# Moving the output bank's evacuation from two half copies on ACT to one copy on ACT and three moves on POOL

## The chip, the cores and the metric

The kernel runs on one core of one Trainium2 chip. The metric is the device time of one execution in microseconds (us), lower is better. Engines are named as the profile names them: PE (matmuls) with PEld (its weight loads), DVE, ACT, POOL, and SP, which issues most DMAs.

## The reference

Three stages follow each other. The first is attention inside clusters, for 2 batches, 8 heads, 768 positions and 64 dimensions per head; the other two are feed-forward layers (512 to 2048 to 512) on the 1536 tokens that come out of it.

```python
q_assign = np.argmax(np.einsum('bhsd,hcd->bhsc', q_n, c_n), axis=-1)   # 16 centroids a head
k_assign = np.argmax(np.einsum('bhsd,hcd->bhsc', k_n, c_n), axis=-1)
mask = q_assign[:, :, :, None] == k_assign[:, :, None, :]
scores = scale * np.matmul(q, k.transpose(0, 1, 3, 2))
scores = np.where(mask, scores, -1000000000.0)
attn = np.exp(scores - np.max(scores, axis=-1, keepdims=True))
attn = attn / (np.sum(attn, axis=-1, keepdims=True) + 1e-09)
x = np.matmul(attn, v)                       # to (tokens, heads * dims)
h = x @ w_in;    x = (h * np.cos(h)) @ w_out
h = x @ w2_in;   y = np.where(h >= 1, h, np.where(h <= -1, 0, (h + 1)**2 / 4)) @ w2_out
```

## The kernel before

Numbers are kept to more than one matmul pass of precision by splitting each fp32 operand into a high part and a low part, so most results are sums of two or three matmuls.

**Pairs, units and slots.** The attention stage works on 8 pairs `i` (a batch and two neighbouring heads). A pair has four units `u = 4 i + 2 h + hf` (head `h`, half `hf` of the 768 query rows), and a unit has six slots, one for each block of 128 keys: 192 slots in all. In its slot a unit transposes the exponentials of one key block on PE (`p_transpose`, L521), ACT copies the high part (`phi`, L524) and DVE makes the low part (`plo`, L529). The scores run `LEAD` = 8 slots ahead: two matmuls per slot (L475, L478), every second slot a row maximum on DVE (`nm`, L484) and an exponential on ACT (`p`, L493). The product with V (`p_v`, L539 and L540) accumulates in the single PSUM bank of `ps_o`; the six blocks are multiplied in the slots 4, 4, 5, 6, 7 and 8 after the unit's first.

**The output bank.** V is stacked as [high | low] for head 0 and [low | high] for head 1, so 64 rows of the bank hold the high product (`main`) and 64 the low one (`other`). After a unit's last product, `o_parts` copies each half on ACT into `xt0` and `xt1`, at the rows of that head (L553). The next unit cannot start its product until both copies have run, as the bank is the only one. After the second head, `finish` (two slots later) transposes the broadcast reciprocals `rb` on PE into `r` (L563), adds `xt0` and `xt1` on POOL (L565), multiplies by `r` on DVE (L566), and POOL splits the product into `xh` (L569) and, two slots later, `xl` (L573). `inverse` (L503 to L508) makes the reciprocals of a unit's sums and spreads each of three columns over 64 columns of `rb` with one POOL instruction a column.

**Preparation of a pair.** `prep_pair(i)` is a generator; the slot loop takes one step of it per slot. Its steps are: transposes of q and k (L331), copies of them on ACT and splits on POOL (L339, L303, L304), DMAs on SP that stack them for the scores (L317), the products with the centroids (L369, L370), their sum (L358), and the argmax chain: maximum (L416), compare (L418), weighting on POOL (L419), maximum (L424), compare (L426). The last step splits V on POOL (L439, L440), transposes the one-hot result on PE into `po` (L449), copies it on ACT (`oht`, L451) and puts eight DMAs on SP (L294) that write it into the stacked operands. The last step runs 5 slots after the previous pair's first; the first step 12 slots before that pair's first slot, because `PREP` is 12 and the generator takes 17 steps to get there.

**Shared buffers and order.** `pt`, `r`, `po`, `ptq` and `pd` all take their PSUM banks from a ring of three (`ps_t`). The order on each engine is not the order of the program text: a scheduler places every instruction from its own estimate of durations, by program order among those that it thinks ready, so the order of the neighbours shifts when a step is moved. `later(n, f)` calls `f` at the n-th next slot boundary.

**The feed-forward layers** take over PE as soon as the last product of the attention stage is done. Their SBUF pool takes the space of the attention pool, so its first writers wait for the last readers of that pool; the second weight block is converted in a chain over ACT, DVE and POOL (L144 to L160) into that space.

Of the kernel before, what the change touches and what calls it, by code (L numbers as in the profile page):

```python
# [8 lines left out]
F32 = mybir.dt.float32  # L9
# [4 lines left out]
AF = mybir.ActivationFunctionType  # L14
ALU = mybir.AluOpType
# [3 lines left out]
P = 128  # L19
# [13 lines left out]
def attention_moe_moe(  # L33
# [18 lines left out]
    nc = tc.nc  # L52
    B, H, S, D = q.shape
# [4 lines left out]
    HJ = NJ // 2  # L58
    HS = S // 2
# [9 lines left out]
    cpool = ctx.enter_context(tc.tile_pool(name="cpool", bufs=1))  # L69
# [2 lines left out]
    desc = cpool.tile([P, C], F32, name="desc")  # L72
    for c in range(C):
        nc.gpsimd.memset(desc[:, c:c + 1], float(C - c))
    ones = cpool.tile([P, D], F32, name="ones")
    nc.gpsimd.memset(ones, 1.0)
    ohscale = cpool.tile([P, 1], F32, name="ohscale")
    ohbias = cpool.tile([P, 1], F32, name="ohbias")
    for r in range(4):
# [25 lines left out]
    def later(n, f, *args):  # L105
        due.setdefault(now[0] + n, []).append((f, args))
# [85 lines left out]
    with ExitStack() as actx:  # L192
        ap = actx.enter_context(tc.tile_pool(name="apool", bufs=1))
# [19 lines left out]
        def ins(x):  # L213
            return x.ins if hasattr(x, "ins") else x

        def run_idle(n, after=None):

            with tc.issue_after(after) if after is not None else ExitStack():
                for _ in range(n):
                    nc.tensor.matmul(idle_o, idle[:, :P], idle, start=True, stop=True)  # L220
# [57 lines left out]
        def prep_pair(i):  # L278
# [3 lines left out]
            t = nat[i][0]  # L282
            if i in (1, 3, 5):
                t2 = w0pool.tile([P, 2, 2, S], F32R, tag="w_0", name=f"t2_{i}")
# [78 lines left out]
            for s in range(2):  # L363
                pd = ps_t.tile([P, NJ, 2, 2, C], F32, tag="t", name=f"pd{i}_{s}")
                for j in range(NJ):
                    cols = slice(j * P, (j + 1) * P)
                    o = pd[:, j].rearrange("p t h c -> p (t h c)")
# [11 lines left out]
            if i == 0:  # L379
                run_idle(NIDLE[2], ins(mm))  # L380
                for s in range(2):
                    dv = dotv[s]
                    m = mx[:, s * G // 2:(s + 1) * G // 2].rearrange("p (j h) -> p j h", h=2)
                    e = eq[:, s * G // 2:(s + 1) * G // 2].rearrange("p (j h) c -> p j h c", h=2)
                    mb = m.unsqueeze(3).to_broadcast([P, NJ, 2, C])
                    db = desc.unsqueeze(1).unsqueeze(1).to_broadcast([P, NJ, 2, C])
                    nc.vector.tensor_reduce(m, dv, AX.X, ALU.max)
                    nc.vector.tensor_tensor(e, dv, mb, ALU.is_ge)
                    nc.vector.tensor_tensor(e, e, db, ALU.mult)
                    nc.vector.tensor_reduce(m, e, AX.X, ALU.max)  # L390
                    nc.vector.tensor_tensor(dv, e, mb, ALU.is_equal)

                    po = ps_t.tile([P, HJ, P], F32, tag="t", name=f"po0_{s}")
                    for jp in range(HJ):
                        mm = nc.tensor.transpose(
                            po[:4 * C, jp],
                            dv[:, 2 * jp:2 * jp + 2].rearrange("p r h c -> p (r h c)"), ident)
                    run_idle(NIDLE[3 + s], ins(mm))
                    last_po[0] = ins(mm)
                    for h in range(2):  # L400
                        for par in range(2):
                            r0 = par * 2 * C
                            dst = st[h][s][D:D + 2 * C, 1].rearrange(
                                "c (jp par n) -> c jp par n", par=2, n=P)[:, :, par]
                            src = po[r0:r0 + 2 * C]
                            if s == 0:
                                nc.scalar.activation(dst, src, AF.Copy)
                            else:
                                nc.vector.tensor_scalar(
                                    dst, src, own[r0:r0 + 2 * C, 0, h:h + 1],  # L410
                                    own[r0:r0 + 2 * C, 1, h:h + 1], ALU.mult, ALU.add)
            else:
                dv = dots.rearrange("p j s h c -> p (j s h) c")
                mb = mx.unsqueeze(2).to_broadcast([P, G, C])
                yield
                nc.vector.tensor_reduce(mx, dv, AX.X, ALU.max)  # L416
                yield
                nc.vector.tensor_tensor(eq, dv, mb, ALU.is_ge)  # L418
                nc.gpsimd.tensor_tensor(  # L419
                    eq, eq, desc.unsqueeze(1).to_broadcast([P, G, C]), ALU.mult)  # L420
                yield
                yield
                yield
                nc.vector.tensor_reduce(mx, eq, AX.X, ALU.max)  # L424
                yield
                nc.vector.tensor_tensor(dv, eq, mb, ALU.is_equal)  # L426
                yield
            if i == 0:
                with tc.issue_after(ins(last[0])):
# [22 lines left out]
            for h in range(2):  # L452
                for s in range(2):
                    for par in range(2):
                        r0 = par * 64 + s * 32 + h * C
                        dst = st[h][s][D:D + C, 1].rearrange(
                            "c (jp par n) -> c jp par n", par=2, n=P)[:, :, par]
# [41 lines left out]
        def inverse(u):  # L499

            i, h, hf = units[u]
            den = dens.pop(u)
            nc.gpsimd.tensor_scalar(den[:, :, 0], den[:, :, 0], 1e-9, 1.0, ALU.add, ALU.mult)  # L503
            nc.vector.reciprocal(den[:, :, 1], den[:, :, 0])
            if h == 0:
                rb[(i, hf)] = ap.tile([P, HJ, 2, D], F32, tag="rb", bufs=2, name=f"rb{i}_{hf}")
            for jj in range(HJ):
                nc.gpsimd.tensor_scalar(rb[(i, hf)][:, jj, h], ones, den[:, jj, 1:2], 1.0,  # L508
                                        ALU.mult, ALU.mult)

        dens = {}
        rb = {}
        pts = {}
        xt = {}
# [29 lines left out]
        def o_parts(u):  # L544
            i, h, hf = units[u]
            o = opsum.pop(u)
            main = slice(h * D, (h + 1) * D)
            other = slice((1 - h) * D, (2 - h) * D)
            if h == 0:
                xt[(i, hf)] = [ap.tile([P, HS], F32, tag=f"xt{n}", bufs=2,  # L550
                                       name=f"xt{n}_{i}_{hf}") for n in range(2)]
            for t, rows in zip(xt[(i, hf)], (main, other)):
                nc.scalar.activation(t[main], o[rows], AF.Copy)  # L553
            if h == 1:
                later(2, finish, i, hf)

        def finish(i, hf):
            b, hp = pairs[i]
            t1, t2 = xt.pop((i, hf))
            r = ps_t.tile([P, HS], F32, tag="t", name=f"r{i}_{hf}")  # L560
            rbt = rb.pop((i, hf))
            for jj in range(HJ):
                nc.tensor.transpose(r[:, jj * P:(jj + 1) * P],  # L563
                                    rbt[:, jj].rearrange("p h d -> p (h d)"), ident)
            nc.gpsimd.tensor_tensor(t1, t1, t2, ALU.add)  # L565
            nc.vector.tensor_tensor(t2, t1, r, ALU.mult)  # L566
            c0 = b * S + hf * HS
            hi, lo = xh[:, hp, c0:c0 + HS], xl[:, hp, c0:c0 + HS]
            nc.gpsimd.tensor_scalar(hi, t2, 1.0, 0.0, ALU.mult, ALU.add)  # L569
            later(2, x_lo, lo, t2, hi)  # L570
# [4 lines left out]

        LEAD, PREP, PREP1 = 8, 12, -3
        PV_AT = (4, 4, 5, 6, 7, 8)
        NSLOT = len(units) * NJ  # L580
        PAIR = 4 * NJ
# [5 lines left out]
        for _ in prep_pair(0):  # L587
            next_slot()
# [9 lines left out]
        for slot in range(-max(LEAD, PREP), NSLOT + PV_AT[-1] - NJ + 1):  # L598
            g = slot + LEAD
            if slot in prep_at:  # L600
                preps.append(prep_pair(prep_at[slot]))
            if 0 <= slot < NSLOT:
                p_transpose(slot // NJ, slot % NJ)
            if 0 <= g < NSLOT:
                scores(g // 2, g % 2)
            for u, kt in pv_slots.get(slot, ()):
                p_v(u, kt)
            if slot % 2 == 0:
                for s in (slot - 1, slot):
                    if 0 <= s < NSLOT:  # L610
                        p_lo(s // NJ, s % NJ)
                if 2 <= g < NSLOT + 2:
                    row_exp(g // 2 - 1)
            next_slot()
            if slot == 60:
                issue_chunk(0)
            preps = [p for p in preps if next(p, 0) != 0]
            if NSLOT - 6 * CHUNK <= slot < NSLOT and slot % 3 == 0:
                pump(1)
            if slot % 2 == 1 and 0 <= g < NSLOT:  # L620
                row_max(g // 2)
# [142 lines left out]
```

## Time and profile before

| | us |
|---|---|
| median of 3 runs | 817.66 (817.46 to 817.7) |
| the profiled execution | 818.13 |
| its span, first to last instruction | 816.1 |
| PE busy in the span | 797.6 (98%) |
| DVE busy | 634.0 (78%) |
| ACT busy | 416.2 (51%) |
| POOL busy | 271.6 (33%) |

Some 2.0 us of the execution lie outside the span. PE's busy time is made of records whose ends are modelled, and neighbouring matmuls overlap in them, so 98% does not say that PE runs at its peak. The row of PEclk shows the TensorE clock that was granted, and the mean over the span is 0.998 of full speed. The shares are means over two very different stages, attention up to about 282 us and the feed-forward layers behind it.

### The profile page before, as it was taken

Reading aid. Unit: us, or ns where it says so; the run is one execution under the profiler, and the core shown is the slowest. Engines: PE = TensorE matmul, PEld = TensorE weight load, DVE = VectorE, ACT = ScalarE, POOL = GpSimd, SP = SyncE. Lnnn points to the kernel's source line nnn. Section 1 sums busy time; section 2 is a strip of 40 time slices with the busy share of each in tenths; the row PEclk is TensorE's granted clock in tenths of the full one; section 3 lists DMA queues with packets and bytes.
Section 4 is the critical chain, followed back from the end, with each engine's and each line's share of the span. In section 5 each row is a group of like instructions: output and inputs, shape, how many; then the busy total and the mean of one; then the engine's idle time right before and its main releaser. Section 6 shows DMA issues by size and latency. Waiting matters only on the chain.

```text
span 816.1 us, 11333 instructions
## 1 busy us (share of the span) xinstructions
PE 797.6 (98%) x4041; PEld 665.9 (82%) x4042; DVE 634.0 (78%) x957; ACT 416.2 (51%) x794; POOL 271.6 (33%) x442
## 2 busy tenths in 40 slices
PE   8899999999999999999999999999999999999998
PEld 4888988988988878888888888888888888888886
DVE  6888899899998596777878778888876987755552
ACT  3778888887888674443343434223444333222220
POOL 3356655675554331222212111342231122111110
PEclk9999999999999999999999999999999999999999
DMA  7865655556440011231222222221122121000012
GB/s 156 203 119 121 154 130 137 110 119 136 115 121 1 1 52 53 103 102 54 67 88 55 101 82 73 61 95 53 52 73 82 59 89 60 1 1 0 14 52 91
DMA packets 48183, 65.97 MB, mean 81 GB/s; under 512 B 27904, under 2 KB 32640, under 8 KB 48128
## 3 DMA queue, kind: packets, MB, share of 16 engines
q1 hardware_dynamic: 47984, 65.22, 29.6%
q8 instruction: 32, 0.52, 0.3%
q14 instruction: 23, 0.19, 0.1%
q10 hardware_dynamic: 144, 0.03, 0.0%
HBM read 43.02 MB, written 3.15 MB: 57 GB/s over the span
## 4 chain that ended last, share of the span: by engine, by line
PE 62%; DVE 1%; ACT 1%; POOL 1%; issue 0%; POOLq 0%
PE y L676 11%; PE y L675 11%; PE y L674 11%; PE h L675 10%; PE h L676 10%; PE h L674 10%; DVE gl L636 0%; DVE r L644 0%; POOL gh L632 0%; DVE g L649 0%; ACT L645 0%; ACT r L645 0%; DVE w L160 0%; ACT n L643 0%; POOL xl L573 0%
## 5 line engine op out<-in xcount | busy, mean ns | idle before, releaser
L632 POOL TENSOR_SCALAR gh<-g 128x512 fp32r<-128x512 f32 x96 | 71.1, 741 | 293.0 <-DVE g L663 156.6
L675 PE MATMUL h<-xl,w 128*128 128x512 f32 x384 | 151.4, 394 | 0.0
L674 PE MATMUL h<-xh,w 128*128 128x512 f32 x384 | 151.4, 394 | 0.0
L676 PE MATMUL h<-xh,w 128*128 128x512 f32 x384 | 151.3, 394 | 0.0
L529 DVE TENSOR_TENSOR plo<-pt,phi 128x384 fp32r<-128x384 f32 x192 | 100.1, 549 | 17.2 <-ACT phi L524 16.5
L524 ACT ACTIVATE phi<-pt 128x384 fp32r<-128x384 f32 x192 | 91.8, 494 | 22.8 <-PE pt L521 21.0
L659 ACT ACTIVATE p<-h,mone 128x512 f32<-128x512 f32 x48 | 33.1, 689 | 134.4 <-DVE m L658 134.0
L521 PE MATMUL pt<-ident,p 128*128 128x128 f32 x576 | 96.7, 277 | 3.5 <-ACT oht L451 1.6
L484 DVE TENSOR_REDUCE nm<-s 128x1 f32<-128x768 f32 x96 | 90.7, 947 | 6.4 <-PE s L478 6.1
L493 ACT ACTIVATE p<-s,nm 128x768 f32<-128x768 f32 x96 | 86.8, 905 | 9.9 <-DVE nm L484 9.5
L636 DVE TENSOR_TENSOR gl<-g,gh 128x512 fp32r<-128x512 f32 x96 | 71.1, 742 | 20.2 <-POOL gh L632 15.3
L676 PEld LDWEIGHTS h<-xh,w 128*128 128x128 f32 x384 | 71.8, 187 | 17.7
L675 PEld LDWEIGHTS h<-xl,w 128*128 128x128 f32 x384 | 71.9, 187 | 17.5
L674 PEld LDWEIGHTS h<-xh,w 128*128 128x128 f32 x384 | 71.9, 187 | 17.5
L144 ACT ACTIVATE wx<-wraw 128x1024 f32<-128x1024 f32 x32 | 36.4, 1138 | 95.3 <-DMA wraw<-in_moe_w_in_dram 36.0
L475 PE MATMUL s<-st,st 128*128 128x384 f32 x192 | 78.4, 408 | 4.1 <-ACT p L493 3.5
L521 PEld LDWEIGHTS pt<-ident,p 128*128 128x128 f32 x576 | 69.9, 140 | 12.8 <-ACT oht L451 3.3
L676 PE MATMUL y<-gh,w 128*128 128x512 f32 x192 | 74.8, 390 | 1.2 <-DVE w L160 1.2
L675 PE MATMUL y<-gl,w 128*128 128x512 f32 x192 | 74.8, 390 | 0.0
L713 DVE TENSOR_TENSOR acc<-y,acc 128x512 f32<-128x512 f32 x72 | 49.3, 686 | 32.9 <-PE y L676 32.9
L675 PE MATMUL y<-w,gh 128*128 128x512 f32 x192 | 74.8, 390 | 0.0
L674 PE MATMUL y<-gh,w 128*128 128x512 f32 x192 | 74.8, 390 | 0.0
(120 smaller groups left out, 1643.5 us busy)
## 6 DMA issues: line engine op xcount, KB each, us to landing
wraw<-in_moe_w_in_dram SPq DMA_DIRECT2D x16, 1024.0 KB, 5.2
wraw<-in_moe_w_out_dram SPq DMA_DIRECT2D x16, 1024.0 KB, 4.9
st<-t SPq DMA_DIRECT2D x24, 192.0 KB, 4.1
st<-th SPq DMA_DIRECT2D x9, 384.0 KB, 3.9
st<-tl SPq DMA_DIRECT2D x18, 192.0 KB, 4.0
st<-th SPq DMA_DIRECT2D x18, 192.0 KB, 3.8
nat<-in_q_dram SPq DMA_DIRECT2D x8, 384.0 KB, 5.4
nat<-in_k_dram SPq DMA_DIRECT2D x8, 384.0 KB, 5.2
```

Of the source, the lines that this page charges most:

```text
L475: nc.tensor.matmul(s[:, step, :HS], qt[:, 0, cols], kt[:, 0, kc], start=True, stop=False)
L484: nc.vector.tensor_reduce(nm, s[:, :, :HS], AX.XY, ALU.max, negate=True)
L493: nc.scalar.activation(p, s[:, :, :HS], AF.Exp, bias=nm, accum_out=dens[u][:, jj, 0:1])
L521: nc.tensor.transpose(ps[:, jj * P:(jj + 1) * P], p[:, kt * P:(kt + 1) * P], ident)
L524: nc.scalar.activation(hi, ps, AF.Copy)
L529: nc.vector.tensor_tensor(lo, ps, hi.bitcast(F32), ALU.subtract)
L632: nc.gpsimd.tensor_scalar(hi, g, 1.0, 0.0, ALU.mult, ALU.add)
L636: nc.vector.tensor_tensor(lo, g, hi.bitcast(F32), ALU.subtract)
L674: nc.tensor.matmul(o, lh, rh, start=first, stop=False)
L675: nc.tensor.matmul(o, lh, rl, start=False, stop=False)
L676: nc.tensor.matmul(o, ll, rh, start=False, stop=last)
L713: nc.vector.tensor_tensor(a, po, a, ALU.add)
```

## The change

Four things change together.

1. `o_parts` copies the whole bank with one ACT instruction of 128 partitions, for either head, into `xt0` (head 0) or `xt1` (head 1).
2. A new function `o_rows`, one slot after the second head's copy, brings the halves to their rows with three POOL instructions of 64 partitions and 384 columns, two of which move data by 64 partitions, and adds them on POOL. `finish` comes three slots after that and no longer adds, so it runs two slots later than before, counted from `o_parts`.
3. `inverse` fills `rb` with one POOL instruction of 192 columns from a broadcast operand, in place of three of 64 columns. The tile `ones` and its memset are gone.
4. The argmax chain gets one more slot between the POOL weighting and the second maximum, and two more between the second compare and the last step. `PREP` and `PREP1` move every pair's preparation three slots earlier, so that the last step stays in its slot.

```diff
-    ones = cpool.tile([P, D], F32, name="ones")
-    nc.gpsimd.memset(ones, 1.0)
...
                 yield
                 yield
                 yield
+                yield
                 nc.vector.tensor_reduce(mx, eq, AX.X, ALU.max)
                 yield
                 nc.vector.tensor_tensor(dv, eq, mb, ALU.is_equal)
+                yield
+                yield
                 yield
...
-            for jj in range(HJ):
-                nc.gpsimd.tensor_scalar(rb[(i, hf)][:, jj, h], ones, den[:, jj, 1:2], 1.0,
-                                        ALU.mult, ALU.mult)
+            nc.gpsimd.tensor_scalar(
+                rb[(i, hf)][:, :, h], den[:, :, 1].unsqueeze(2).to_broadcast([P, HJ, D]),
+                1.0, 0.0, ALU.mult, ALU.add)
...
-            if h == 0:
-                xt[(i, hf)] = [ap.tile([P, HS], F32, tag=f"xt{n}", bufs=2,
-                                       name=f"xt{n}_{i}_{hf}") for n in range(2)]
-            for t, rows in zip(xt[(i, hf)], (main, other)):
-                nc.scalar.activation(t[main], o[rows], AF.Copy)
+
+            t = ap.tile([P, HS], F32, tag=f"xt{h}", bufs=2, name=f"xt{h}_{i}_{hf}")
+            xt.setdefault((i, hf), []).append(t)
+            nc.scalar.activation(t, o, AF.Copy)
             if h == 1:
-                later(2, finish, i, hf)
+                later(1, o_rows, i, hf, main, other)
+
+        def o_rows(i, hf, main, other):
+            t0, t = xt[(i, hf)]
+            t2 = ap.tile([P, HS], F32, tag="xt2", bufs=2, name=f"xt2_{i}_{hf}")
+            xt[(i, hf)] = (t, t2)
+            for dst, rows, src in ((t2, other, t0[main]), (t2, main, t[other]), (t, other, t0[other])):
+                nc.gpsimd.tensor_scalar(dst[rows], src, 1.0, 0.0, ALU.mult, ALU.add)
+            nc.gpsimd.tensor_tensor(t, t, t2, ALU.add)
+            later(3, finish, i, hf)
...
-            nc.gpsimd.tensor_tensor(t1, t1, t2, ALU.add)
             nc.vector.tensor_tensor(t2, t1, r, ALU.mult)
...
-        LEAD, PREP, PREP1 = 8, 12, -3
+        LEAD, PREP, PREP1 = 8, 15, -6
```

## Rows read from the trace of the kernel before

**Rows 1.** The page, busy us, share of the span and instructions of each engine.

```profile
PE 797.6 (98%) x4041; PEld 665.9 (82%) x4042; DVE 634.0 (78%) x957; ACT 416.2 (51%) x794; POOL 271.6 (33%) x442
```

**Rows 2.** Windows: length, each engine's busy us and instructions, clock, DMA share, GB/s.

```profile
0.00:38.00 38.00, 33.05 (x191) 24.21 (x193) 28.43 (x70) 20.45 (x45) 14.77 (x55) 0.96 0.79 171
38.00:282.00 244.00, 235.19 (x1555) 211.47 (x1554) 214.47 (x369) 205.50 (x456) 139.41 (x246) 1.00 0.47 109
282.00:816.10 534.10, 529.33 (x2299) 430.20 (x2297) 391.08 (x519) 190.29 (x294) 117.41 (x141) 1.00 0.19 62
...
160.70:194.00 33.30, 31.59 (x214) 28.77 (x213) 31.75 (x54) 28.21 (x63) 23.05 (x39) 1.00 0.53 114
```

**Rows 3.** The chain that ended last, in order of time: start, us, what.

```profile
282.07 1.03 POOL xt L565
...
285.42 0.60 ACT n L643
...
304.77 1.22 DVE w L160
306.04 0.50 PE y L676
```

**Rows 4.** Timeline 157 to 168.5 us: start, us, instruction [idle before, releaser].

```profile
157.81 0.49 PE L521 MATMUL pt<-ident,p 128*128 128x128 f32 x3
...
158.85 0.49 PE L521 MATMUL pt<-ident,p 128*128 128x128 f32 x3
...
160.09 0.98 ACT L553 ACTIVATE xt<-o 64x384 f32<-64x384 f32 x2 [0.16 <-PE o L540]
...
160.39 0.34 PE L478 MATMUL s<-st,st 80*128 80x384 f32 x1
...
161.12 0.44 PE L539 MATMUL o<-phi,vv 128*128 128x384 f32 x1 [0.39 <-ACT xt L553]
...
164.38 0.88 DVE L426 TENSOR_TENSOR dots<-eq,mx 128x384 f32<-128x384 f32 x1
...
165.97 0.67 ACT L451 ACTIVATE oht<-po,ohbias,ohscale 128x384 fp32r<-128x384 f32 x1 [1.07 <-PE po L449]
...
166.69 0.64 PEld L521 LDWEIGHTS pt<-ident,p 128*128 128x128 f32 x6 [0.51 <-ACT oht L451]
...
167.96 0.19 PEld L475 LDWEIGHTS s<-st,st 128*128 128x128 f32 x1 [0.47 <-ACT p L493]
```

**Rows 5.** Waits 38 to 282 us: who for whom, us in total, times, longest.

```profile
PEld o L539 <- ACT xt L553: 7.6, 17, 0.7
PEld s L475 <- ACT p L493: 7.5, 19, 0.6
...
PEld pt L521 <- ACT oht L451: 3.3, 7, 0.5
...
PE o L539 <- ACT xt L553: 2.4, 7, 0.4
```

**Rows 6.** Instructions by line and shape to 300 us: count, busy us, mean ns, idle before.

```profile
L529 DVE TENSOR_TENSOR plo<-pt,phi 128x384 fp32r<-128x384 f32 x192 | 100.1, 549 | 17.2 <-ACT phi L524 16.5
...
L553 ACT ACTIVATE xt<-o 64x384 f32<-64x384 f32 x64 | 31.0, 485 | 2.9 <-PE o L540 2.1
L508 POOL TENSOR_SCALAR rb<-ones,den 128x64 f32<-128x64 f32 x96 | 30.6, 338 | 5.8 <-DVE den L504 5.8
...
L565 POOL TENSOR_TENSOR xt<-xt,xt 128x384 f32<-128x384 f32 x16 | 16.9, 1058 | 24.9 <-ACT xt L553 24.9
...
L303 POOL TENSOR_SCALAR t<-t 128x384 fp32r<-128x384 f32 x8 | 4.1, 515 | 2.9 <-ACT t L339 2.7
...
L314 POOL TENSOR_SCALAR st<-th 64x768 fp32r<-64x768 f32 x2 | 1.7, 830 | 0.2
...
L418 DVE TENSOR_TENSOR eq<-dots,mx 128x384 f32<-128x384 f32 x7 | 5.7, 808 | 0.0
```

**Rows 7.** Waits of SP's queue, 38 to 282 us.

```profile
SPq L317 <- PE s L478: 78.3, 12, 10.0
```

## The prediction

> **What bounds the kernel now.** I read the page's busy shares first [rows 1]: PE has 797.6 of 816.1 us, so anything that does not shorten or unblock PE is worth nothing by itself. The change adds and removes no matmul. What it can move is time in which PE waits.
>
> The windows split that by stage [rows 2]. From 282 us to the end PE is busy 529.33 of 534.10 us: the feed-forward layers are PE's own work, and the change has no instruction there. From 38 to 282 us PE is busy 235.19 of 244.00 us, and ACT 205.50 and DVE 214.47 beside it: three engines near their limit, PE in front. The gain has to come from this stage. Before 38 us PE lacks 4.95 us (38.00 - 33.05).
>
> The timeline says what an undisturbed slot costs and what a disturbed one does [rows 4]. Two neighbouring transposes of a slot start at 157.81 and 158.85: 1.04 us a slot. At 160.39 the last score matmul starts, and the next product only at 161.12, 0.73 us later; ordinarily the next matmul of this size starts some 0.18 us behind (half of the 0.34 us that its record lasts). So 0.55 us are lost. PE's own idle before it is given as 0.39 us, because the matmul's record runs long; PEld's row in the waits has up to 0.7 us for one such wait [rows 5]. PEld's sums are therefore nearer the truth than PE's (for this wait 7.6 us against 2.4 us), and I price stalls by them.
>
> Three waits of PE on ACT stand out [rows 5]: for the output bank 7.6 us in 17 times, for the exponential that frees a score bank 7.5 us in 19, for the one-hot copy `oht` that frees a bank of the ring 3.3 us in 7. Together 18.4 us.
>
> The chain of waits adds one thing [rows 3]: it runs through the end of the attention stage. The last POOL add at 282.07 leads to the first activation of the next stage at 285.42, which waits for the old pool's space, and the chain goes on through the second weight block to the DVE instruction at 304.77 and the matmul at 306.04. So the tail behind the last product is on the path, and what makes it longer makes the kernel longer.
>
> **One copy in place of two on ACT.** Before: 64 copies of 64 x 384, 485 ns each, 31.0 us [rows 6]. A copy's time follows its columns: 64 partitions and 384 columns cost ACT the 485 ns, and 128 partitions would have to differ from that for no reason that a row gives. On POOL 64 x 768 costs 830 ns and 128 x 384 515 ns [rows 6], which again follows columns and not partitions. After: 32 copies at 0.49 us, 15.6 us. ACT loses 15.4 us of its 205.50. More to the point, the bank comes free 0.49 us sooner, 32 times. A wait of mean 7.6 / 17 = 0.45 us vanishes; one of 0.7 us keeps 0.2 us. I count 6.5 of the 7.6 us as removable.
>
> **The longer argmax chain.** In the example the second compare runs on DVE from 164.38 to 165.26, ACT stands idle 1.07 us until the transposes of its result are there, copies `oht` at 165.97, and PE waits 0.51 us for the ring and then 0.47 us more for an exponential that ACT reached late [rows 4]. Before, one slot lies between the compare and the transposes, after it three; the weighting gets four slots in place of three. With two more slots of 1.04 us the compare has 2.1 us more, above the 1.07 us of idle. Removable: the 3.3 us and, behind each of the 7, the 0.47 us, 3.3 us again; 6.6 us. The bound below is nothing, if DVE simply runs the compare as late as before: the scheduler may still place it last.
>
> **The rest of the waits for exponentials.** 7.5 - 3.3 = 4.2 us. ACT is relieved of four copies a pair, some 1.9 us in 33.3, and I count a third, 1.4 us, as removable (nothing to 4.2).
>
> Sum of what can be removed: 6.5 + 6.6 + 1.4 = 14.5 us.
>
> **How much of it reaches the end.** PE cannot run faster than its inputs, and behind ACT stands DVE: in the window of one pair, 160.7 to 194.0 us, DVE is busy 31.75 of 33.30 us, PE 31.59 and ACT 28.21 [rows 2]. In such a pair only 1.55 us can go before DVE is full; over the stage DVE leaves 29.5 of 244 us. A wait taken from ACT is thus partly given back as a wait for `plo` or `nm`. Between nothing and all of 14.5 us I take 45%, 6.5 us, or 0.9 us in each of some 7.4 pairs: that is within the 1.55 us of the fullest pair.
>
> **POOL's moves and fills.** Removed: 96 fills of 64 columns at 338 ns, 30.6 us, and 16 adds that only change place [rows 6]. Added: 32 fills of 192 columns and 48 moves of 64 x 384. No row shows a fill from a broadcast operand or a POOL move between partitions. The fill lies between 338 ns (64 columns) and 515 ns (384 columns): I take 0.36 us, 11.5 us in all. The move lies between 515 ns and the 1058 ns of the dearest POOL instruction of this width, the add; I take 0.52 us since cost follows columns, 25.0 us in all. POOL gets 5.9 us more, on 139.41 of 244.00: hidden by 104 us of idle time. The new tile and the missing memset cost nothing: the memset stands in the head start, ahead of any data.
>
> **The tail.** Behind the last product the old way is two copies, an add, the product, `xh`, `xl`. The new one saves 0.49 us of ACT and adds moves: three at 0.52 us, or two if the first, which reads the first head's tile alone, is run before. That is +0.55 to +1.07 us, up to +2.7 us at 1.06 a move. I take +0.6. It adds to PE's wait at 306.04 in full, as that matmul already waits.
>
> **Moved steps.** `finish` is two slots later: its transposes take a ring bank at a slot's start where `po` no longer follows at once, and `xh`, `xl` are wanted by the feed-forward layers only, more than a pair away except in the tail above. The `rb` tile of the next pair is now asked for one slot before the transposes that free its buffer; POOL's fill waits at most 1.04 us for them, with `xh`, `xl` and V's split behind it, 7 times, and the fills are read 12 slots later: hidden while POOL idles 43% of the stage. Preparation three slots earlier also moves ten stacking DMAs, two loads of q and k and their PE and ACT work. On SP the stacking DMAs of the second head wait for a buffer that the scores free (78.3 us, up to 10.0 at once [rows 7]); that moment stays, so the wait grows by three slots, some 3.1 us, and what is queued behind (V's load and the eight one-hot DMAs) keeps its time. If SP's cover failed, PE's scores would wait for one landing; PE has no such wait in the list behind [rows 5]. In the head start, preparing pair 1 earlier competes with the first scores within PE's 4.95 us of idle: I take nothing, between -1 and +1.5 us.
>
> **Sum** against the profiled execution: 818.13 - 6.5 + 0.6 = 812.2 us. The median of the runs is 0.5 us below that execution, so 811.8 us.
>
> **The rivals.**
>
> *All of it comes through.* DVE's instructions lie loosely enough, as in other pairs they must: over the stage it has 12% idle. Then 817.66 - 14.5 + 0.6 = 803.8 us. Against it stands the pair with 1.55 us of room.
>
> *The waits only change their name.* DVE or the scheduler's new order takes back what ACT gives: 817.66 + 0.6 and up to 1 us either side for a new order, 816.5 to 819.3 us. For it: DVE's window; and that I cannot see the order which the scheduler will draw.
>
> *POOL is late (slower).* The chain from bank to product is now copy 0.49, three moves, add 1.01 to 1.06 us and some 0.3 us between them, before DVE may multiply, and DVE runs in order: its multiply at `finish` would hold `plo` and `nm` behind it, and `r` would hold a ring bank. From `o_parts` to `finish` there are four slots, 4.2 us at 1.04. With 0.52 us a move the chain takes 3.4 us. It decides from moves of 0.77 us on, or from a backlog on POOL of 0.8 us. At 1.06 us a move the chain is 5.0 us, 0.8 us late, 16 times, 13 us; with the tail at +2.7 and the gain of 6.5 us, 817.66 + 13 + 2.7 - 6.5 = 826.9 us, and 819.5 if half of that is hidden. POOL's idle 104 us speaks against a steady backlog; that no row shows a move across partitions speaks for it.
>
> *Contention between DVE and POOL.* The first compare of the argmax chain takes 808 ns where the `plo` of the same shape takes 549 [rows 6]; both run on DVE, and the first has both operands in SBUF. If a POOL move held each of the 14 compares for its 0.52 us, DVE would have 7.3 us more; at the same 45% 3.3 us reach PE, and the time is 815.1 us. The Trainium skill, "SBUF — State Buffer", section "Who interferes with whom", says that a DVE instruction with two SBUF inputs contends with a POOL instruction that reads SBUF, and that the second to issue waits for the first. The 808 ns agree with it; that the moves will hit the compares, no row shows, since POOL's load hardly grows.
>
> **How the numbers follow.** A difference of 0.2%, 1.6 us, is about what a measurement of this kernel can tell from none. Chances: forecast 0.52, all comes through 0.12, waits change their name 0.17, POOL late 0.13, contention 0.06. The forecast's own range is 807.5 (75% of 14.5) to 815.4 us (20%). For the whole I go to 805.0 below, nearer to the full gain, and to 818.5 above, which leaves out POOL's case and the top of the unchanged one, and about a twentieth below. Faster by over 0.2%: 0.52 + 0.12 + 0.06 = 0.70. Within 0.2%: 0.16 of the 0.17. Slower: 0.13 and 0.01, 0.14.
>
> **What the profile after would show.** Right: 32 copies on ACT at 0.49 us; PEld's wait for the bank near 1 us; the wait for `oht` near nothing, and no idle of ACT before it; moves at 0.5 us; the last add some 0.6 us later behind the last product; the stage from 38 us shorter by 6 us. Wrong: moves near 1 us, DVE idle before its multiply for POOL, waits of PE for `plo` in place of those for ACT, or a start that reaches its first product late.

## The result and the profile after

The changed kernel takes 826.75 us (median, 825.09 to 828.0), the kernel before 817.6: a ratio of 1.0105, 95% interval 1.0092 to 1.0117. (The ratios are estimated from the runs; the quotient of two medians can differ from them by up to 0.001.) The forecast of 811.8 us and its range, 805.0 to 818.5 us, are missed, and the sign is wrong.

The windows of the changed kernel, cut at the end of its attention stage (columns as in [rows 2]), say where:

```profile
0.00:38.00 38.00, 32.21 (x190) 24.25 (x192) 29.49 (x72) 21.23 (x46) 14.87 (x52) 1.00 0.83 174
38.00:289.50 251.50, 234.75 (x1557) 209.57 (x1557) 212.08 (x367) 189.78 (x423) 148.13 (x231) 1.00 0.45 105
289.50:824.00 534.50, 529.51 (x2297) 429.79 (x2295) 390.88 (x519) 190.42 (x294) 118.63 (x144) 1.00 0.18 62
```

The feed-forward layers take what they took before (534.50 against 534.10 us), and the first 38 us hold about the same matmuls (190 against 191) [rows 2]. The attention stage is 7.5 us longer (251.50 against 244.00), although PE, DVE and ACT are all busy for less of it: ACT by 15.7 us, where 15.4 were forecast. Only POOL has more, 8.7 us, where 5.9 were forecast. So PE, DVE and ACT all wait more, which points to a chain of waits and not to a load.

The waits from 38 to 292 us (who for whom, us in total, times, longest) show which waits went and which came:

```profile
DVE den L505 <- POOL den L504: 24.4, 18, 2.0
PE pt L522 <- DVE plo L530: 14.9, 16, 1.4
ACT p L494 <- DVE nm L485: 14.5, 15, 1.9
...
PEld pt L522 <- DVE plo L530: 10.9, 15, 1.6
...
PEld pt L522 <- issue: 8.3, 6, 1.7
...
PEld o L540 <- ACT xt L553: 3.4, 12, 0.3
...
PEld s L476 <- ACT p L494: 2.3, 9, 0.5
```

Before, from 38 to 282 us, the first three of these pairs were:

```profile
ACT p L493 <- DVE nm L484: 7.1, 17, 1.1
...
DVE den L504 <- POOL den L503: 4.2, 7, 1.0
...
PE pt L521 <- DVE plo L529: 1.3, 3, 0.8
```

PE's waits for ACT went the way that the prediction said (PEld's rows): the bank from 7.6 to 3.4 us, the exponential from 7.5 to 2.3, and the wait for `oht`, 3.3 before [rows 5], is not in the list any more. The sum falls from 18.4 to 5.7 us, by 12.7 of the 14.5 that were counted. In their place PE waits for `plo` on DVE, 14.9 us against 1.3, and DVE waits 24.4 us, 18 times, for one small POOL instruction: L504, which adds 1e-9 to three columns of row sums (the tile `den`) ahead of DVE's reciprocal. Before, the same two instructions (L503, L504 there) made DVE wait 4.2 us. Of PEld's idle time 8.3 us stand under `issue`, where the profile shows no releaser; all six of them end 0.03 us ahead of the end of a wait of PE for `plo`, so they belong to the same stalls.

The timeline around a pair's start (157 to 176 us) shows such a wait whole:

```profile
159.08 1.39 POOL L562 TENSOR_SCALAR xt<-xt 64x384 f32<-64x384 f32 x2 [6.37 <-ACT xt L553]
...
160.56 1.01 POOL L563 TENSOR_TENSOR xt<-xt,xt 128x384 f32<-128x384 f32 x1
...
161.52 1.01 POOL L417 TENSOR_TENSOR eq<-eq,desc 128x384 f32<-128x384 f32 x1
...
162.62 0.20 POOL L504 TENSOR_SCALAR den<-den 128x3 f32<-128x3 f32 x1
...
162.85 0.18 DVE L505 RECIPROCAL den<-den 128x3 f32<-128x3 f32 x1 [1.81 <-POOL den L504]
162.94 0.93 DVE L485 TENSOR_REDUCE nm<-s 128x1 f32<-128x768 f32 x1
...
163.79 1.01 DVE L530 TENSOR_TENSOR plo<-pt,phi 128x384 fp32r<-128x384 f32 x2
163.90 0.90 ACT L494 ACTIVATE p<-s,nm 128x768 f32<-128x768 f32 x1 [1.89 <-DVE nm L485]
...
164.48 0.52 PE L522 MATMUL pt<-ident,p 128*128 128x128 f32 x3 [1.43 <-DVE plo L530]
...
172.67 0.18 DVE L505 RECIPROCAL den<-den 128x3 f32<-128x3 f32 x1 [2.03 <-POOL den L504]
```

POOL runs two moves, the add and the argmax weighting with pauses of under 0.1 us, and only then the 0.20 us addition. DVE reaches its reciprocal 1.81 us too early and, since it runs in order, a row maximum and two `plo` whose inputs are there (the scores by 160.63, the copies `phi` by 162.01) stand behind it. Those leave ACT idle for 1.89 us and PE for 1.43 us. Ten us later the same happens with 2.03 us on DVE, as the last line shows. The chain of waits between those two (start, us, what) is POOL's queue:

```profile
165.34 0.51 POOL xh L577
...
165.94 0.68 POOL xl L581
...
166.90 0.53 POOL vv L440
...
167.50 0.86 POOL xt L562
...
168.43 1.01 POOL vv L441
169.44 0.48 POOL xt L562
...
170.40 0.98 POOL xt L563
171.38 0.97 POOL vv L441
...
172.43 0.21 POOL den L504
...
172.67 0.04 DVE den L505
```

Over the kernel the instructions cost about what was forecast (groups by line and shape, to 300 us; columns as in [rows 6]):

```profile
L562 POOL TENSOR_SCALAR xt<-xt 64x384 f32<-64x384 f32 x48 | 27.3, 569 | 47.7 <-ACT xt L553 44.9 <-DMA st<-oht 0.2
...
L553 ACT ACTIVATE xt<-o 128x384 f32<-128x384 f32 x32 | 15.8, 494 | 3.1 <-PE o L541 3.1
...
L508 POOL TENSOR_SCALAR rb<-den 128x192 f32<-128x192 f32 x32 | 12.4, 387 | 12.3 <-DVE den L505 9.5 <-PE r L572 2.7
...
L416 DVE TENSOR_TENSOR eq<-dots,mx 128x384 f32<-128x384 f32 x7 | 4.5, 640 | 0.0
```

### The profile page after: what moved, and what is told of

It is laid out like the page before. It is cut to its first block, busy times and chain, and to the rows that moved or that the text cites. A ratio compares the mean times of both kernels' runs of the same rounds, so it can differ in the third digit from the quotient of the medians.

```text
span 824.0 us, 11275 instructions
## 1 busy us (share of the span) xinstructions
PE 796.5 (97%) x4041; PEld 663.6 (81%) x4042; DVE 632.5 (77%) x957; ACT 401.4 (49%) x762; POOL 281.6 (34%) x425
## 4 chain that ended last, share of the span: by engine, by line
PE 76%; POOL 9%; DVE 6%; ACT 4%; issue 2%; DMA 1%; SPq 0%; POOLq 0%; ACTq 0%; DVEq 0%
PE y L684 10%; PE y L683 10%; PE y L682 10%; PE h L682 10%; PE h L683 10%; PE h L684 10%; PE pt L522 4%; PE s L476 2%; PE o L540 2%; PE s L479 2%; PE o L541 2%; DVE plo L530 2%; POOL xt L562 2%; ACT p L494 1%; POOL xt L563 1%
## 5 line engine op out<-in xcount | busy, mean ns | idle before, releaser
L522 PE MATMUL pt<-ident,p 128*128 128x128 f32 x576 | 100.5, 278 | 16.4 <-DVE plo L530 15.5
L476 PE MATMUL s<-st,st 128*128 128x384 f32 x192 | 80.2, 417 | 2.1 <-ACT p L494 2.1
L683 PE MATMUL y<-w,gh 128*128 128x512 f32 x192 | 74.8, 390 | 0.0
L682 PE MATMUL y<-w,gh 128*128 128x512 f32 x192 | 74.7, 389 | 0.0
```

The lines of the kernel that those rows point to most:

```text
L476: nc.tensor.matmul(s[:, step, :HS], qt[:, 0, cols], kt[:, 0, kc], start=True, stop=False)
L522: nc.tensor.transpose(ps[:, jj * P:(jj + 1) * P], p[:, kt * P:(kt + 1) * P], ident)
L682: nc.tensor.matmul(o, lh, rh, start=first, stop=False)
L683: nc.tensor.matmul(o, lh, rl, start=False, stop=False)
```

## The experiments

Theory A: the moves lengthen POOL's queue, the addition stands in it, and DVE waits for it in its order. Rival B: the preparation three slots earlier costs, by itself or by the order of instructions that follows from it. Rival C: the moves cost by POOL's load or by holding up DVE's reads.

**Without the addition, in the changed kernel and in the one before.**

```diff
-            nc.gpsimd.tensor_scalar(den[:, :, 0], den[:, :, 0], 1e-9, 1.0, ALU.add, ALU.mult)
```

> The changed kernel without the POOL instruction that adds 1e-9 to the row sums (left out: that addition), so DVE's reciprocal waits for ACT's sums and for nothing on POOL. Theory A (the reciprocal waits in DVE's order for an addition that stands on POOL behind the new moves; plo and PE wait behind it): DVE's wait before the reciprocal falls from 24.4 us to under 5, PE's wait for plo from 15.5 us to under 5, the time from 826.75 to 808 to 816 us. Rival B (the preparation three slots earlier, or the order of instructions that follows from it, costs the time): 822 us or more. Rival C (the moves load POOL or hold up DVE's reads directly): 820 us or more.

> The kernel before without the same addition (left out: + 1e-9 on the sums). Theory A: DVE waited only 5.0 us for it there, mostly not on PE's path, so 814 to 817.6 us; the same edit is worth under 4 us here and over 10 in the changed kernel. Rivals B and C say nothing of it; if it were worth as much here as there, the wait would not be the change's doing.

Changed kernel: 808.54 us, ratio to before 0.9883 (0.9866 to 0.9899). Kernel before: 816.73 us, 0.9987 (0.9977 to 0.9997). The same 32 small instructions are worth 18.2 us in the one and 0.7 in the other (817.46 less 816.73; the kernel before took 817.46 us beside these runs). In the changed kernel without them (waits of DVE, 38 to 280 us) the reciprocal waits 2.6 us for ACT's sums, and PE's wait for `plo` is 1.8 us:

```profile
DVE den L504 <- ACT p L494: 2.6, 7, 0.6
```

Theory A holds, B and C fall as the main cause.

**Without the moves.**

```diff
-            for dst, rows, src in ((t2, other, t0[main]), (t2, main, t[other]), (t, other, t0[other])):
-                nc.gpsimd.tensor_scalar(dst[rows], src, 1.0, 0.0, ALU.mult, ALU.add)
-            nc.gpsimd.tensor_tensor(t, t, t2, ALU.add)
+            nc.gpsimd.tensor_tensor(t, t, t0, ALU.add)
```

> The changed kernel without the three POOL moves (left out: bringing the halves to their rows; the add stays and sums the two copies as they lie). POOL has some 25 us less. Theory A and rival C: the addition reaches DVE sooner, 811 to 818 us, DVE's wait before the reciprocal under 12 us. Rival B: 822 us or more.

817.85 us, 0.9998 (0.9987 to 1.001), at the upper end of what was expected. DVE's wait for the addition (38 to 300 us) is 10.1 us in place of 24.4:

```profile
DVE den L505 <- POOL den L504: 10.1, 16, 1.1
```

So the moves lengthen the queue, at a price of 8.9 us; but some of the wait stays without them, more than the 4.2 us of the kernel before.

**The old argmax chain in the changed kernel.** The diff is the reverse of the part of the change with `yield`, `PREP` and `PREP1`.

> The changed kernel with the argmax chain, PREP and PREP1 as before. Theory A and rival C: still slower than before, 821 to 829 us, with over 15 us of DVE's wait before the reciprocal. Rival B: 818 us or less.

838.56 us, 1.0261 (1.0233 to 1.0289): slower still, and above theory A's range as well, DVE's wait 27.0 us. Rival B falls for the change as a whole: going back to the later preparation costs 11.8 us more. This wait, only 2.6 us longer, does not explain those 11.8 us; the table below shows that half of them, 5.9, come without the addition too.

**All the work, but the reciprocal, and the fill of `rb` behind it, two slots later.**

```diff
             nc.gpsimd.tensor_scalar(den[:, :, 0], den[:, :, 0], 1e-9, 1.0, ALU.add, ALU.mult)
+            later(2, invert, u, den)
+
+        def invert(u, den):
+            i, h, hf = units[u]
             nc.vector.reciprocal(den[:, :, 1], den[:, :, 0])
```

> The changed kernel with all its work, but the reciprocal and the fill of rb two slots after the addition on POOL in place of right behind it. If what costs is DVE waiting in its order (theory A), the wait before the reciprocal falls from 24.4 us to under 8 and the time to 807 to 815 us, near the 808.5 of the run without the addition. If the 32 additions cost by their own load on POOL or by holding DVE's reads (rival C), it stays at 822 us or more.

811.16 us, 0.9915 (0.9897 to 0.9932). POOL's work is as in the changed kernel; the reciprocal has another place in DVE's order and the fill another on POOL. The wait is (waits of DVE, 38 to 280 us):

```profile
DVE den L509 <- POOL den L504: 5.5, 7, 1.1
```

This separates the wait from the work: 15.6 us go with nothing taken away. The two places were moved together, so the fill's share is not separated.

**The kernel before with three idle moves per add.**

```diff
+            ex = ap.tile([P, HS], F32, tag="xt2", bufs=2, name=f"xt2_{i}_{hf}")
+            for rows, src in ((slice(0, D), t1[0:D]), (slice(D, P), t2[D:P]), (slice(0, D), t2[0:D])):
+                nc.gpsimd.tensor_scalar(ex[rows], src, 1.0, 0.0, ALU.mult, ALU.add)
             nc.gpsimd.tensor_tensor(t1, t1, t2, ALU.add)
```

> The kernel before with three more POOL moves of 64 x 384 into a tile that nobody reads, ahead of each of the 16 adds of the output halves; ACT's two copies stay. Theory A: POOL's queue alone makes DVE wait for the addition: its wait rises from 5.0 us to 12 or more and the time to 821 to 832 us. If only the combination with the earlier preparation costs (rival B), 817 to 820 us.

827.14 us, 1.0108 (1.0092 to 1.0124): the time as expected, the place not. Theory A had put at least 12 us at the addition. The moves stand here right ahead of the add that DVE's multiply needs, and the waits of DVE (38 to 300 us) rise at the multiply, from 3.2 us in 2 times to 7.4 in 9, more than at the addition, from 4.2 to 5.7:

```profile
DVE xt L569 <- POOL xt L568: 7.4, 9, 3.3
DVE den L504 <- POOL den L503: 5.7, 7, 1.3
```

So a longer queue on POOL also makes DVE wait at another of its results, the one that the rival "POOL is late" had named. The two rises, 5.7 us together, are less than the 9.5 us that the time grows by; the rest is not traced.

**The argmax chain alone, with and without the addition, and the rest without it.**

> The kernel before with the longer argmax chain and PREP, PREP1 of the change alone. The prediction's term: PE's wait for oht (3.3 us) and the exponential behind it (3.3 us) go, 45% of it reaches the end: 812 to 816 us. Rival B (the earlier preparation costs): 819 us or more.

> The kernel before with the new argmax chain, PREP and PREP1, and without the addition on POOL (left out: + 1e-9). The chain alone cost 5.8 us. If that ran through DVE's wait for the addition (7.5 us there against 5.0), this is 811 to 817 us; if it runs through the two copies on ACT, which PE waits for longer (10.0 us against 7.6), 819 to 823 us.

> The changed kernel without the addition on POOL (left out: + 1e-9) and with the argmax chain, PREP and PREP1 as before. With the addition the old chain gave 838.6 us, 12 more than the new one. If those 12 us ran through the same wait (theory A alone), this is 808 to 813 us; if the old chain costs by itself because POOL's weighting and the transposes of the one-hot come late behind the moves, 815 to 824 us.

The first: 823.36 us, 1.0068 (1.0047 to 1.009), outside the range of the prediction's term and inside rival B's: on the kernel before, the term that was to save some 3 us costs 5.8. The second: 818.9 us, 1.0024 (1.0015 to 1.0033), between its two ranges, 0.1 us below the second. The third: 814.39 us, 0.9955 (0.994 to 0.9969), between its two ranges. Together with the runs above they make a table of medians, us:

| | with the addition on POOL | without it |
|---|---|---|
| neither part | 817.6 | 816.73 |
| argmax chain alone | 823.36 | 818.9 |
| copy, moves, fill alone | 838.56 | 814.39 |
| all (the change) | 826.75 | 808.54 |

In neither column do the parts add up: without the addition the chain costs 2.2 us on the old kernel and saves 5.9 behind the single copy. Along the rows, the addition costs 0.9, 4.5, 24.2 and 18.2 us; in the change without the moves it costs 7.0 (817.85 against the 810.9 below). So the moves are the larger part of what makes the addition dear, but not all: the argmax chain alone raises its price as well, and what the fill and the later product add was not separated.

In the run with the chain alone the wait for `oht` falls from 3.3 to 1.4 us (PEld's rows; PE's own list has none), as forecast, but the wait for the bank grows from 7.6 to 10.0 us by PEld's rows, and PE's own rows show more for the bank (2.4 before) and for `plo` (1.3 before):

```profile
PE pt L524 <- DVE plo L532: 4.2, 8, 0.7
PE o L542 <- ACT xt L556: 3.4, 12, 0.7
```

**Neither the addition nor the moves.**

> The changed kernel without the addition and without the three moves (left out: + 1e-9, and bringing the halves to their rows). Theory A: once DVE does not wait in POOL's queue, the moves are hidden but for the tail, so 806 to 809 us, near the 808.5 with them. If the moves cost beside that wait (rival C): 802 us or less.

810.9 us, 0.9926 (0.9911 to 0.9941), above theory A's range and 2.4 us slower than with the moves, but far from the 802 us of rival C. Once nothing on DVE waits for POOL's addition, the moves cost nothing that shows; the 2.4 us I put down to the order that the scheduler draws, and did not test it.

**The addition on DVE, and on ACT.**

```diff
-            nc.gpsimd.tensor_scalar(den[:, :, 0], den[:, :, 0], 1e-9, 1.0, ALU.add, ALU.mult)
+            nc.vector.tensor_scalar(den[:, :, 0], den[:, :, 0], 1e-9, 1.0, ALU.add, ALU.mult)
```

> The changed kernel with all its work, the addition of 1e-9 made by DVE itself right before its reciprocal. Theory A: no wait for POOL is left, DVE gets 32 small instructions of some 0.18 us more (5.8 us, of which 0.06 to 0.1 us each show since neighbours overlap): 808.5 to 812 us. If POOL's load were the cost (rival C): 820 us or more.

817.04 us, 0.9998 (0.9989 to 1.0007), a miss of theory A's range: no semaphore wait for POOL is left before the reciprocal, and yet 8.5 us more than without the addition. The view of that line gives 154 ns at the least, 224 in the middle and 1799 at most for one instruction of three columns:

```profile
L504 DVE TENSOR_SCALAR den<-den x32: 154/224/1799, 25.9 to 273.5; 128x3 f32<-128x3 f32 x32
```

The timeline of that kernel around the longest:

```profile
164.99 1.01 POOL L563 TENSOR_TENSOR xt<-xt,xt 128x384 f32<-128x384 f32 x1
...
165.19 1.80 DVE L504 TENSOR_SCALAR den<-den 128x3 f32<-128x3 f32 x1
...
165.95 1.01 POOL L441 TENSOR_TENSOR vv<-natv,vv 128x384 fp32r<-128x384 f32 x1
...
166.91 0.54 DVE L530 TENSOR_TENSOR plo<-pt,phi 128x384 fp32r<-128x384 f32 x1
...
167.37 0.16 DVE L505 RECIPROCAL den<-den 128x3 f32<-128x3 f32 x1
```

The addition starts while POOL adds, and ends at 166.99, behind POOL's next instruction too (166.96). The fast ones, 0.15 to 0.17 us, stand where POOL is idle, but for one, at 31.14 us, which stands about where the first of two POOL instructions (L441) ends. So in this case DVE was held until the second of two POOL instructions had ended. The next run took the addition off both:

```diff
-            nc.gpsimd.tensor_scalar(den[:, :, 0], den[:, :, 0], 1e-9, 1.0, ALU.add, ALU.mult)
+            nc.scalar.activation(den[:, :, 0], den[:, :, 0], AF.Copy, bias=1e-9)
```

> The changed kernel with all its work, the addition of 1e-9 made by ACT behind the exponential that ends the sums. In the run with the addition on DVE it took DVE 154 ns where POOL was idle and up to 1799 ns where POOL was running, each long one ending 20 to 40 ns behind the end of a POOL instruction; that run came to 817.0 us. If that hold-up of DVE behind POOL was the cause there, ACT, which showed no such long copies, makes the addition for some 0.2 us, 32 times 0.2 = 6.4 us of its time, and the kernel takes 808.5 to 812 us. If an addition between the sums and the reciprocal costs wherever it stands, 815 us or more.

811.17 us, 0.9923 (0.9909 to 0.9937), as expected and with all the work in it. ACT takes 199 to 260 ns for it. This and the run with the late reciprocal beat both kernels; the run without the addition is faster still, and as every sum holds an exponential of 0, which is 1, the 1e-9 is below the last bit of an fp32 sum (argued, not measured).

## Why the prediction was wrong

**The bound: right. The price of a stall: not settled.** PE was held by waits in the attention stage. That PEld's sums price a stall better than PE's own was not tested, and the traces do not decide it. In the changed kernel the last product starts 7.5 us later, and all waits of the stage grow by 8.3 us on PE and by 9.8 on PEld. In the changed kernel without the addition it starts 9.2 us earlier than before, and the waits shrink by 5.0 us on PE and by 7.5 on PEld. By PE's own rows the three waits that the prediction priced are 6.0 us (2.4, 2.0 and 1.6) in place of 18.4.

**One copy on ACT: right.** 494 ns for 128 partitions, as for 64; ACT lost 15.7 us of its stage (15.4 forecast); the bank's wait fell by 4.2 us where 6.5 had been counted.

**The rest of the waits for ACT: right in sum.** 12.7 us of the counted 14.5 are gone.

**POOL's moves and fills: the step that failed.** It priced each instruction well (a move 0.57 us in the mean against 0.52, a fill 0.39 against 0.36) and then put their effect at nothing, as POOL's 5.9 us more are "hidden by 104 us of idle time". What the runs showed in its place is DVE's wait for the addition behind that work, 24.4 us against 4.2, which costs 18.2 us of time; 15.6 of them came back with all the work kept. POOL's idle time lies elsewhere: at a pair's start its queue runs with pauses of at most 0.1 us, from 165.34 to 172.43 in the example. What had to be asked is what else stands on POOL behind the moves and who waits for it. The answer was in the code, in `inverse`: the addition, and DVE's reciprocal right behind it.

**The rival "POOL is late": right side, wrong place, and its size by luck.** It gave 819.5 to 826.9 us, and 826.75 came out. But it let DVE wait at the multiply, which waited only once, 4.0 us in the tail, and its upper end was worked out with moves of 1.06 us, where 0.51 (the median) came. Its lower end does not follow from its sum either: half of the 13 us, with the other terms as they stand, gives 820.4. With a chance of 0.13 it was held too low for a queue whose contents had not been listed. Of its two conditions, moves of 0.77 us and a backlog on POOL, the backlog came about, at another instruction.

**The rival "the waits only change their name": the name right, the price not.** PE's waits for ACT did come back as waits for `plo`, but as DVE's wait for POOL and not as DVE being full, and 826.75 us lie above its 816.5 to 819.3.

**The longer argmax chain: its mechanism right, its worth wrong.** In the change the `oht` wait went, but alone the chain costs 5.8 us, and 2.2 where the addition is gone too. It saves time only together with the single copy, 5.9 us without the addition; that this is because the bank comes free sooner is not shown. Terms that were added up are not independent.

**45% of the gain reaching the end: near in its result.** With the addition's wait cut short and all the work in, the change is worth 6.4 us (late reciprocal) or 6.5 (addition on ACT), against 5.9 forecast. In part two errors cancel: of the three waits for ACT 12.0 and 12.4 us are gone there by PEld's rows, not 14.5, and more than half of that reached the end.

**The tail: right in sign.** The last product starts at 280.53 of 816.1 us before and at 288.02 of 824.0 after: 535.6 and 536.0 us behind it, +0.4 us for +0.6.

**Contention at the compares: wrong.** The first compare fell from 808 to 640 ns [rows 6]. Contention between DVE and POOL came up elsewhere, when the addition was put on DVE.

Still open: why the chain alone costs 2.2 us on the old kernel without the addition, which part of the change beside the moves lengthens the wait for the addition, and why the run without the moves and the addition is 2.4 us above the one with the moves. Each edit also makes the scheduler draw another order, and that was not held fixed.

## What to carry to other kernels

Work that goes to a half idle engine is not free: list what stands behind it on that engine's queue at that moment, and who waits for each result, the smallest first. A 0.2 us instruction whose consumer runs in order on a full engine can carry the whole queue onto the path; move the consumer later, or the small instruction to the engine that makes its input. And test the parts of a change together as well as alone: here two parts that each lost or gained little alone gave 8 us together (by the right column of the table), once the small wait was gone.

## What the runs showed of the hardware

A DVE `tensor_scalar` of 128 x 3 fp32, SBUF to SBUF, took 154 ns with POOL idle and up to 1799 ns with POOL running, ending 20 to 40 ns behind the end of a POOL instruction, in the four longest (1.70 to 1.80 us) the second in a row. The reciprocal of the same three columns behind it took 159 to 178 ns throughout, also where POOL was running (at 31.94 and 61.31 us). The Trainium skill, "SBUF — State Buffer", section "Who interferes with whom", says that `tensor_scalar` can, on fitting operands, enter a mode that takes the ports which DVE shares with POOL, and that the one which comes second then waits for the whole instruction of the other. The trace agrees. Where two POOL instructions followed each other closely, DVE was held through both in those four cases, and in three others (at 60.49, 90.98 and 156.91 us) it ended 20 to 30 ns behind the first, with the second begun; what decides between the two is open.

POOL is held up as well: in the changed kernel its addition of 128 x 3, 199 ns in the middle, took 1.06 us at 109.89, while DVE ran an instruction with two tensor inputs (L149) from 109.00 to 110.88.

A POOL move between partitions 64 apart costs no more than one without: the 48 moves of 64 x 384, two thirds of them shifted, take 504 ns at the least and 509 in the middle, against 515 for 128 x 384 in place [rows 6]. Their mean of 569 ns comes from longer ones, up to 938.
